# The bounds of a query tile as a stream of their own, and new allowances, in a planned kernel of attention and long convolution

## The chip, the cores and the metric

One core of one Trainium2 chip runs the kernel. The metric is the device time of one execution in microseconds; the time before is 1150.65 us, the median of three runs (1150.41 to 1154.25). TensorE is written PE, VectorE DVE, ScalarE ACT, GpSimd POOL and SyncE SP in the rows.

## The reference, cut to what matters

Two independent layers stand side by side in the output. The first is a state space convolution over 2048 positions and 576 channels, whose kernel is made from 128 complex exponentials per channel. The second is attention with 32 query heads of 18 rows and one key and value head.

```
def _A_ref(u, A_re, A_im, B_re, B_im, C_re, C_im, log_dt, Dskip):
    ...
    P = jnp.exp(logdA[:, :, None] * l[None, None, :])
    K = jnp.einsum("dn,dnl,dn->dl", Cc, P, dB).real
    ...                                   # y = irfft(rfft(u) * rfft(K)), causal, in float32
    y = y.transpose(0, 2, 1) + u * Dskip[None, None, :]

def _B_ref(x, wq, wk, wv, wo):
    q = (x @ wq).reshape(B, S, H, Dh).transpose(0, 2, 1, 3)
    k = x @ wk
    v = x @ wv
    scores = jnp.einsum("bhqd,bkd->bhqk", q, k) * (Dh ** -0.5)
    p = _softmax(scores, axis=-1)
    o = jnp.einsum("bhqk,bkd->bhqd", p, v)
    return o.transpose(0, 2, 1, 3).reshape(B, S, H * Dh) @ wo

return jnp.concatenate([a, b], axis=-1)
```

## The kernel before, in words

**Attention is the main line.** The 2048 queries are cut into 4 chunks `c` of 512 columns. A group `g` is four heads, two pairs; a chunk has eight groups. For each pair and each of 16 key blocks `kb` a score tile `s` of 128 keys by two heads by 512 queries is made by TensorE (`scores`, L516), ScalarE makes the exponential `P` of it (L527; L525 for the first group, with a bias), and a product with the values adds it to the output bank `ops` (L823). There are 1024 such tiles. `main` walks over them in rounds of three, because there are three score tiles (`NS`) in PSUM: in each round it emits three scores, three exponentials, and one or two products of two tiles each, which lag behind; ten `P` tiles (`NP`) lie between. At the end of a group VectorE copies `ops` to `o` (`gather`, through the helper at L123), and the first product of the next group has to wait for that copy, since there is one output bank. The 1024 tiles make 342 rounds, and 32 groups have 31 ends that wait in this way.

**Side work of attention.** A query tile (c, m) holds the projected queries of up to seven heads. `qproj` (matmuls at L408, bank `q`) makes it, and VectorE writes it as two half precision parts `qh` and `ql`; `queries` stores both to DRAM (`qd`) by nine or so DMAs on POOL's queue (L458). Then follows the bound of the tile: a small matrix `aw`, matmuls into the bank `up` (L193), the maximum `un`, its running maximum, and the shift `sh`, which POOL stores too (L496). `fetch` lets SyncE bring the finished operands `aug` of a head pair back from DRAM (L505); the scores of the pair wait for them. There are 20 tiles; the first one, and the key side, are made in `setup`. At the end of a chunk the output is scaled and projected (`outproj`, bank `op`; in the last chunk in parts, bank `part` and `finish`).

**Convolution.** The 576 channels are worked through in 12 blocks `k`. For each block a front stream (VectorE tables `tab`, matmuls `kg`, copy `ksb`) and a back stream (transforms `hu`, `lu`, `hk`, `lk` on TensorE, long products `us`, `ks`, `acc` on VectorE, inverse transform `iy`, L119 is the helper of most of the VectorE work). A back stream runs beside the next front stream. In three places of the program (`powers`, "bursts") ScalarE loads other tables and evaluates sines on `stage` for the following blocks, and makes no exponentials of scores meanwhile.

**What sets the order.** All orders on TensorE, VectorE and ScalarE are written out when the program is built, by a planner with a clock of its own (`Clock`): it counts assumed costs for TensorE (`t`), VectorE (`v`) and ScalarE (`a`). The side work, the preparation of outputs and the convolution are Python generators (`Stream`), which yield a kind, an earliest time, and whether they hold the one bank `f` that all side matmuls share. Kind "p" is matmul work, "v" VectorE work, "w" waits for a condition, "b" is a burst that waits for other side work or 16 steps. After the scores of a round `main` gives it a credit of time, and `fill` lets streams spend it, in a set order of preference, until the next score tile is free by the planner's clock. Constants steer this: `RATE` and `PACE` say how much convolution work a step should have seen, `TOTAL` and `LAST` how much filling is spread over how many steps, `GAP`, `DEFER`, `SLACK`, `HEAD`, `LEFT` shift single decisions. In the kernel before a query tile and its bound are one generator (`yield from self.queries(...)`), so a tile's bound comes before the next tile's projection.

Of the kernel before, what the change touches and what calls it, by code (L numbers as in the profile page):

```python
# [9 lines left out]
F32 = mybir.dt.float32  # L10
# [7 lines left out]
P = 128  # L18
# [12 lines left out]
HQ = (0, 7, 14, 21, 28, 32)  # L31
# [11 lines left out]
NS = 3  # L43
NP = 10


RATE = 1.84
PACE = 1.79
AHEAD = 0.7
TOTAL = 340.0  # L50
LAST = 500

GAP = 0.4
DEFER = 0.5
NAUG = 5
SLACK = 3.0
HEAD = 12

LEFT = 0.85

LATE = {1: [0], 3: [1], 5: [2], 6: [3]}

# [133 lines left out]
class Attention:  # L196
# [36 lines left out]
    def setup(self, tp, conv):  # L233
# [48 lines left out]
        self.outs, self.step, self.due, self.scaled = [], 0, 1 << 30, {}  # L282
        self.o_left = self.q_left = self.units = 0
        self.todo, self.busy, self.group = [], False, 0
        self.side_work = Stream(self.side(), self.k, 99.0)
        conv.begin(6)
        p1, small = (self.ps_s.tile([P, 2, CT], F32, tag="s", name=n) for n in ("first", "small"))
# [21 lines left out]
                queries(p1, j, k)  # L309
            project(p1, 3, 0, 0, k)  # L310
        nc.scalar.activation(h1, p1, AF.Copy, scale=QS)
        self.ab0 = ab = self.p2.tile([P, 2], F32, tag="ab", name="ab0_0")
        V.tensor_reduce(ab[:, 0:1], p1, axis=AX.X, op=ALU.max, apply_absolute_value=True)
        V.scalar_tensor_tensor(l1, p1, QS, h1, op0=ALU.mult, op1=ALU.subtract)
        V.tensor_scalar(ab[:, 0:1], ab[:, 0:1], QS, None, op0=ALU.mult)
# [78 lines left out]
    def qproj(self, c, m, xt):  # L394

        nc, V, K = self.nc, self.V, self.k
        w, nf = self.wq[m], 2 if m < 4 else 1
        self.q_left = 5 * nf
        yield "p", K.fill, False
        ps = self.bank(CT, f"q{c}_{m}")  # L400
        for f in range(nf):
            for k in range(5):
                for j in range(4):

                    o = slice(32 * j, 32 * j + 32)
                    i = o if m < 4 else slice(32 * (j % 2), 32 * (j % 2) + 32)
                    x = slice(256 * f, 256 * f + 256) if m < 4 else slice(256 * (j // 2), 256 * (j // 2) + 256)
                    nc.tensor.matmul(ps[o, 256 * f:256 * f + 256], w[:, k, i], xt[:, k, x], start=(k == 0), stop=(k == 4), tile_position=(0, 32 * j))  # L408
                K.pe(0.465)
                self.q_left -= 1  # L410
                self.units += 1
                if (f, k) != (nf - 1, 4):
                    yield "p", 0.0, True
        self.conv_wait()
        qh, ql, ab = self.operands(c, m)
        n = 256 * nf
        V.tensor_scalar(qh[:, :n], ps[:, :n], QS, None, op0=ALU.mult)
        V.scalar_tensor_tensor(ql[:, :n], ps[:, :n], QS, qh[:, :n], op0=ALU.mult, op1=ALU.subtract)
        K.filled()
        V.tensor_reduce(ab[:, 0:1], qh[:, :n], axis=AX.X, op=ALU.max, apply_absolute_value=True)  # L420
        yield from self.queries(c, m, qh, ql, ab)

    def conv_wait(self):
        self.k.v = max(self.k.v, self.k.t)
# [1 line left out]
    def operands(self, c, m):  # L426
        return (self.p2.tile([P, CT], F16, tag="qh", name=f"qh{c}_{m}", bufs=1),
                self.p2.tile([P, CT], F16, tag="ql", name=f"ql{c}_{m}", bufs=1),
                self.p2.tile([P, 2], F32, tag="ab", name=f"ab{c}_{m}"))

    @staticmethod
    def pieces(m, h0):
# [10 lines left out]
    def queries(self, c, m, qh, ql, ab):  # L443

        nc, V, K = self.nc, self.V, self.k
        h0, h1 = HQ[m:m + 2]
        if m == 0:
            self.qd[c] = self.dr.tile([H, 55, CT], F16, tag="qd", name=f"qd{c}")
        qd = self.qd[c]

        n0 = 4 if (c, m) == (0, 0) else 0

        def store(q):
            for row, src in ((0, qh), (18, qh), (36, ql)):
                for i, h, n, d, nd in self.pieces(m, n0):
                    for f in range(1 if m < 4 else 2):
                        cs, i1 = (slice(0, CT), i) if m < 4 else (slice(256 * f, 256 * f + 256), i + 64 * f)
                        q.dma_start(qd[h:h + n, row + d:row + d + nd, cs], src[i1:i1 + n * nd, :cs.stop - cs.start])  # L458

        def store_first(q):  # L460
            for row, part in ((0, 0), (18, 0), (36, 1)):
                for i, h, d, nd in ((72, 4, 0, 18), (90, 5, 0, 6), (96, 5, 6, 12), (108, 6, 0, 18), (126, 7, 0, 2)):
                    src = self.parts[part + 2 * (i >= 96)]
                    q.dma_start(qd[h, row + d:row + d + nd, :], src[i:i + nd, :])
        (store_first if n0 else store)(nc.gpsimd)
        yield "v", 0.0, False
        while not self.bounded:
            yield "w", 0.0, False
        aw = self.p2.tile([P, P], F32, tag="aw", name=f"aw{c}_{m}")

        ends = (FLOOR, ALU.max) if n0 else (TOP, ALU.min)
        V.tensor_scalar(aw, ab[:, 0:1].broadcast_to([P, P]), ends[0], self.kmax[:, m:m + 1], op0=ends[1], op1=ALU.mult)

        yield "p", max(K.v + (0.4 if self.due < self.step + 12 else SLACK), K.fill), False

        up = self.bank(8, f"up{c}_{m}")
        matmul4(nc, up, aw, self.sel[:, 8 * m:8 * m + 8], stop=(m == 0))
        if m > 0:
            n = 8 if m == 4 else 4
            for b in range(0, n, 4):  # L480
                matmul4(nc, up[:, b:b + 1], self.aw, self.sel[:, 39 + m:40 + m], start=False, stop=(b + 4 == n))
        self.aw = aw
        K.pe(0.1)
        K.v = max(K.v, K.t + 0.3)
        un = self.p2.tile([P, 1], F32, tag="un", name=f"un{c}_{m}", bufs=4)
        V.tensor_reduce(un, up, axis=AX.X, op=ALU.max)
        K.filled()
        if self.ubound is not None:
            u2 = self.p2.tile([P, 1], F32, tag="u2", name=f"u2_{c}_{m}", bufs=4)
            V.tensor_tensor(u2, un, self.ubound, op=ALU.max)  # L490
# [200 lines left out]
    def side(self):  # L691

        xts = {0: self.x0}
        units = [(c, m) for c in range(NCH) for m in range(5)]
        yield from self.queries(0, 0, None, None, self.ab0)
        for c, m in units[1:]:
            self.due = 16 * (8 * c + (0, 1, 3, 5, 7)[m])
            while self.outs:
# [64 lines left out]
    def main(self, conv, flag):  # L763
        nc, K = self.nc, self.k
# [5 lines left out]
        for st in conv.streams:  # L770
            st.ready = 0.0
        prep = Stream(self.prepare(), K, 99.0)
        pairs = [(c, g, kb, j) for c in range(NCH) for g in range(8) for kb in range(16) for j in range(2)]
        state = dict(credit=0.0, filled=0.0)

# [3 lines left out]
        def force(done):  # L779
            while not done():  # L780
                st = holder()
                (side if st is None else st).advance()
                self.fetch(self.group)

        def fill(then):
# [3 lines left out]
            while more:  # L789
# [1 line left out]
                credit = state["credit"] - (K.t - t - idle)  # L791
                urgent = self.due < self.step + 8
                late = self.late()
                for st in (prep, side, conv) if urgent else (prep, conv, side):

                    if st is side and side.kind == "p" and not (urgent or side.holds) and conv.lags(self.step):
                        continue
                    spare = credit - 0.3 if st is not side or urgent or late or side.holds else 0.0
                    wait = then - K.t - (1.2 if st is side and not urgent and not side.holds and self.units > 0.6 * self.step + HEAD else 0.15)
                    if st.go(self.step, max(spare, wait, 0.3 * (st is side and side.holds and conv.lags(self.step) and credit > -1.0)), holder()):  # L800
                        more = True
                        break
                else:

                    at = min((x for x in (st.event() for st in [prep, side] + conv.streams) if x > K.t), default=then)
                    if at < then - 0.5:
                        idle += at - K.t
                        K.t = at
                        more = True
# [1 line left out]
            if K.t > t:  # L811
                K.t += 0.03
            state["filled"] += K.t - t
            state["credit"] = max(state["credit"] - (K.t - t), -0.8)

        def product(n):
            nonlocal o_ps
# [17 lines left out]
        for r in range(0, len(pairs), NS):  # L835
# [24 lines left out]

                self.load_wo()

            state["credit"] = min(state["credit"] + NS / 2 * (0.88 + min(max((TOTAL - state["filled"]) / max(LAST - s, 20), 0.45), 0.7 if s < 384 else 0.9)), 1.2 + 0.88)

            def free():

# [116 lines left out]
class Conv:  # L983
# [303 lines left out]
    def meanwhile(self):  # L1287

        K = self.k
        while K.v < K.t - GAP:  # L1290
            st = min((st for st in self.streams if st.live and st.kind == "v" and st.ready <= K.v and not st.gen.gi_running),
                     key=lambda st: st.work, default=None)
            if st is None or self.work > self.at.step * RATE + 20.0:
                break
            w0 = K.work
            st.advance()
# [151 lines left out]
    def go(self, step, credit, lock):  # L1448
        self.turn()
        lag = step * RATE - self.work  # L1450
        if lag < -20.0:
            return False
        ahead = AHEAD + min(max(lag, 0.0) / 20.0, 1.0)
        for st in self.streams:
# [121 lines left out]
```

## Time and profile before

| what | us |
|---|---|
| median of 3 runs (lowest, highest) | 1150.65 (1150.41, 1154.25) |
| span of the profiled execution, first to last instruction | 1153.0 |
| busy: TensorE matmuls, VectorE, ScalarE, GpSimd | 1083.5, 987.4, 998.8, 140.6 |
| first exponential of scores starts | 26.87 |
| last exponential of scores ends | 1128.27 |

The page gives no other time for the profiled execution than its span. Busy shares are the union of an engine's instruction times; matmuls overlap each other in their tails, so the busy time of TensorE is more than what its instructions need one after the other. A float32 matmul of the program leaves two records. Rows of an engine carry in square brackets how long it was idle before them and what ended that.

### The profile page before, as it was taken

Reading aid. Unit: us, or ns where it says so; the run is one execution under the profiler, and the core shown is the slowest. Engines: PE = TensorE matmul, PEld = TensorE weight load, DVE = VectorE, ACT = ScalarE, POOL = GpSimd, SP = SyncE. Lnnn points to the kernel's source line nnn. Section 1 sums busy time; section 2 is a strip of 40 time slices with the busy share of each in tenths; the row PEclk is TensorE's granted clock in tenths of the full one; section 3 lists DMA queues with packets and bytes.
Section 4 is the critical chain, followed back from the end, with each engine's and each line's share of the span. In section 5 each row is a group of like instructions: output and inputs, shape, how many; then the busy total and the mean of one; then the engine's idle time right before and its main releaser. Section 6 shows DMA issues by size and latency. Waiting matters only on the chain.

```text
span 1153.0 us, 33012 instructions
## 1 busy us (share of the span) xinstructions
PE 1083.5 (94%) x13886; PEld 395.9 (34%) x13886; DVE 987.4 (86%) x1679; ACT 998.8 (87%) x1052; POOL 140.6 (12%) x257
## 2 busy tenths in 40 slices
PE   6999899989999999989999999999998999999998
PEld 2333233333333334323333333333332333332423
DVE  3697997998997897897799899898699799799694
ACT  2888979879989898998998899988999988899891
POOL 5232320112032000001021200001040000000000
PEclk9899999999999999999999999999999999999999
DMA  7422242114122202112222300202221301301201
GB/s 224 130 57 84 76 133 89 45 41 135 32 67 78 74 29 88 45 63 93 82 79 71 110 21 28 93 28 85 75 78 46 111 20 39 106 19 54 77 33 58
DMA packets 59279, 83.37 MB, mean 72 GB/s; under 512 B 14867, under 2 KB 35335, under 8 KB 58613
## 3 DMA queue, kind: packets, MB, share of 16 engines
q1 hardware_dynamic: 47557, 73.24, 19.4%
q0 software_dynamic: 10848, 7.37, 2.6%
q8 instruction: 111, 1.82, 0.6%
q10 hardware_dynamic: 720, 0.58, 0.2%
q14 instruction: 43, 0.35, 0.1%
HBM read 46.59 MB, written 33.85 MB: 70 GB/s over the span
## 4 chain that ended last, share of the span: by engine, by line
PE 64%; DVE 15%; ACT 14%; issue 5%; DMA 1%; SPq 0%; ACTq 0%; DVEq 0%
PE ops L823 27%; PE s L516 17%; ACT P L527 12%; PE op L193 5%; PE q L408 3%; DVE tab L119 3%; PE kg L1257 3%; PE iy L193 3%; DVE ks L119 1%; DVE acc L119 1%; DVE t L119 1%; PE hk L193 1%; PE fin L193 1%; PE lk L193 1%; DMA xr<-xT 1%
## 5 line engine op out<-in xcount | busy, mean ns | idle before, releaser
L527 ACT ACTIVATE P<-s 128x1024 f32<-128x1024 f32 x992 | 934.8, 1034 | 104.6 <-PE s L516 102.2
L823 PE MATMUL ops<-P,v_sb 128*32 128x512 f32 x4096 | 513.0, 601 | 8.5 <-DVE o L123 8.4
L516 PE MATMUL s<-aug,kaug 55*128 55x512 f16 x2048 | 309.9, 384 | 36.6 <-ACT P L527 30.7
L516 PEld LDWEIGHTS <-kaug 55*128 55x128 f16 x2048 | 92.2, 94 | 371.7 <-issue 328.5
L823 PEld LDWEIGHTS ops<-P,v_sb 128*32 128x32 f32 x4096 | 117.2, 110 | 162.6 <-issue 126.1
L458 POOL DMA_DIRECT2D qd<-qh x116 | 65.7, 573 | 323.2 <-DVE qh L127 320.6
L408 PE MATMUL q<-x,wq_sb 128*32 128x256 f32 x1360 | 84.2, 382 | 3.2 <-DVE sck L119 2.5
L193 PE MATMUL op<-wo_sb,oT 126*32 126x288 f32 (+1 forms) x1048 | 74.8, 410 | 2.6 <-DVE sck L119 1.2
L119 DVE TENSOR_TENSOR tab<-tab,tt 128x576 f32<-128x576 f32 (+1 forms) x72 | 59.1, 821 | 1.4
L123 DVE COPY ksb<-kg 128x192 f32<-128x192 f32 x48 | 17.5, 364 | 49.1 <-PE kg L1257 48.9
L119 DVE TENSOR_TENSOR tt<-fr,sum 128x576 f32<-128x576 f32 (+1 forms) x72 | 58.9, 818 | 0.0
L119 DVE TENSOR_TENSOR tab<-tab 128x576 f32<-128x576 f32 (+1 forms) x72 | 58.9, 818 | 0.0
L119 DVE TENSOR_TENSOR tab<-fr,dif 128x576 f32<-128x576 f32 (+1 forms) x72 | 58.9, 818 | 0.0
L119 DVE TENSOR_TENSOR tab<-sum,fr 128x576 f32<-128x576 f32 (+1 forms) x72 | 58.8, 816 | 0.0
L408 PEld LDWEIGHTS q<-x,wq_sb 128*32 128x32 f32 x1360 | 40.5, 110 | 43.4 <-issue 19.1
L1168 POOL MEMSET fr<- 128x192 f32 x24 | 9.8, 494 | 323.8 <-DVE tt L119 225.2
L119 DVE TENSOR_TENSOR acc<-acc,pt 128x1728 f32<-128x1728 f32 (+2 forms) x36 | 48.7, 1352 | 0.3
L119 DVE TENSOR_TENSOR pt<-us,ks 128x1728 f32<-128x1728 f32 (+2 forms) x36 | 48.2, 1351 | 0.0
L525 ACT ACTIVATE P<-s,bias 128x1024 f32<-128x1024 f32 x32 | 32.7, 1131 | 15.1 <-PE s L516 15.1
L193 PEld LDWEIGHTS op<-wo_sb,oT 126*32 126x32 f32 (+1 forms) x1048 | 29.8, 110 | 42.2 <-issue 17.4
L1257 PEld LDWEIGHTS kg<-tab 128*32 128x32 f32 x2304 | 35.5, 110 | 22.9 <-issue 7.9
L1257 PE MATMUL kg<-tab 128*32 128x64 f32 x2304 | 41.8, 221 | 1.5 <-DVE ksb L123 1.1
(160 smaller groups left out, 1018.0 us busy)
## 6 DMA issues: line engine op xcount, KB each, us to landing
od<-o SPq DMA_DIRECT2D x31, 256.0 KB
aug<-qd SPq DMA_DIRECT2D x124, 55.0 KB
u<-u SPq DMA_DIRECT2D x12, 384.0 KB
kd<-ksb SPq DMA_DIRECT2D x12, 384.0 KB
kt<-kd SPq DMA_DIRECT2D x48, 96.0 KB
outa<-u SPq DMA_DIRECT2D x12, 384.0 KB
pw<-pw SPq DMA_DIRECT2D x8, 528.0 KB
oT<-od SPq DMA_DIRECT2D x16, 252.0 KB
```

The lines of the kernel that those rows point to most:

```text
L119: return self.v.tensor_tensor(out, *a, **k)
L123: return self.v.tensor_copy(out, *a, **k)
L193: nc.tensor.matmul(ps[j:e], w[:, j:e], x, start=start, stop=stop, tile_position=(0, j))
L408: nc.tensor.matmul(ps[o, 256 * f:256 * f + 256], w[:, k, i], xt[:, k, x], start=(k == 0), stop=(k == 4), tile_position=(0, 32 * j))
L458: q.dma_start(qd[h:h + n, row + d:row + d + nd, cs], src[i1:i1 + n * nd, :cs.stop - cs.start])
L516: nc.tensor.matmul(ps[:, j, :], self.kaug[r, kb * P:(kb + 1) * P], t[r, :], start=True, stop=True)
L525: nc.scalar.activation(pt, ps, AF.Exp, bias=self.bias, scale=SCALE / QQ)
L527: nc.scalar.activation(pt, ps, AF.Exp, scale=SCALE / QQ)
L823: nc.tensor.matmul(o_ps[32 * j:32 * j + 32, :], self.v[:, kb, :], pts[2 * n + j // 2][:, j % 2, :], start=(kb == 0), stop=(kb == 15), tile ...
L1168: nc.gpsimd.memset(t[:, :, 0:NF:8], one)
L1257: nc.tensor.matmul(ps[32 * g:32 * g + 32, d, :], t[:, :32], t[:, 32:], start=(j == 0), stop=(j == 1), tile_position=(0, 32 * g))
```

## The change

The bound of a tile leaves `queries` and becomes a method of its own, `bound`. `queries` now only issues the stores and appends the bound to a list, `tails`. A new stream, `tail`, works through this list; the side stream goes on with the next tile. In `fill` the tail stream stands behind the preparation and before side work and convolution, and has a fixed allowance of 1.0. `ab` gets six buffers, as several tiles may wait for their bounds. The pair of convolution streams stays. The constants are set anew, and twelve that stood in the code as numbers become `C1` to `C12` (two lines of the table are shown). The convolution may be 47.793 us of VectorE work ahead of its pace instead of 20.

```diff
-TOTAL = 340.0
-LAST = 500
+TOTAL = 429.151
+LAST = 560.514
...
-        yield from self.queries(c, m, qh, ql, ab)
+        self.queries(c, m, qh, ql, ab)
+        yield "v", 0.0, False
...
         (store_first if n0 else store)(nc.gpsimd)
+        self.tails.append(self.bound(c, m, ab, n0, qd))
+
+    def tail(self):
+
+        while True:
+            if self.tails:
+                yield from self.tails.pop(0)
+            else:
+                yield "w", 0.0, False
+
+    def bound(self, c, m, ab, n0, qd):
+
+        nc, V, K = self.nc, self.V, self.k
+        h0, h1 = HQ[m:m + 2]
         yield "v", 0.0, False
         while not self.bounded:
             yield "w", 0.0, False
...
         def force(done):
             while not done():
                 st = holder()
-                (side if st is None else st).advance()
+                if st is None:
+                    st = tail if self.tails or tail.kind != "w" else side
+                st.advance()
...
-                for st in (prep, side, conv) if urgent else (prep, conv, side):
+                for st in (prep, tail, side, conv) if urgent else (prep, tail, conv, side):
...
-                    spare = credit - 0.3 if st is not side or urgent or late or side.holds else 0.0
-                    wait = then - K.t - (1.2 if st is side and not urgent and not side.holds and self.units > 0.6 * self.step + HEAD else 0.15)
+                    spare = 1.0 if st is tail else credit - C9 if st is not side or urgent or late or side.holds else 0.0
+                    wait = then - K.t - (C6 if st is side and not urgent and not side.holds and self.units > C7 * self.step + HEAD else C8)
...
-            state["credit"] = min(state["credit"] + NS / 2 * (0.88 + min(max((TOTAL - state["filled"]) / max(LAST - s, 20), 0.45), 0.7 if s < 384 else 0.9)), 1.2 + 0.88)
+            state["credit"] = min(state["credit"] + NS / 2 * (0.88 + min(max((TOTAL - state["filled"]) / max(LAST - s, 20), C1), C2 if s < 384 else C3)), C4 + 0.88)
...
         lag = step * RATE - self.work
-        if lag < -20.0:
+        if lag < -C11:
             return False
```

Three places of the orders are shown. The first is VectorE's order near the start, where the queries of tiles 1 and 2 of the first chunk become `qh` and `ql` and the shift `sh` of tile 1 is made. Before:

```order
L127 TENSOR_SCALAR qh_1_627<-q_1_533 128x512
L131 SCALAR_TENSOR_TENSOR ql_1_628<-q_1_533,qh_1_627 128x512
L135 TENSOR_REDUCE ab_1_629<-qh_1_627 128x1
L127 TENSOR_SCALAR aw_1_642<-ab_1_629,kmax 128x128
L119 TENSOR_TENSOR tt_0_0_0_593<-fr_423,sum_542 128x576
L119 TENSOR_TENSOR tab_0_590<-tab_0_590 128x24x24
L135 TENSOR_REDUCE un_1_678<-up_1_669 128x1
L119 TENSOR_TENSOR u_0_1_680<-un_1_678,un_0_499 128x1
L127 TENSOR_SCALAR sh_1_682<-u_0_1_680 8x256
```

Of the change:

```order
L128 TENSOR_SCALAR qh_2_712<-q_2_618 128x512
L132 SCALAR_TENSOR_TENSOR ql_2_713<-q_2_618,qh_2_712 128x512
L136 TENSOR_REDUCE ab_2_714<-qh_2_712 128x1
L136 TENSOR_REDUCE un_1_744<-up_1_735 128x1
L120 TENSOR_TENSOR u_0_1_746<-un_1_744,un_0_584 128x1
L128 TENSOR_SCALAR sh_1_748<-u_0_1_746 8x256
```

The shift of tile 1 has moved from behind its own tile to behind the queries of tile 2. The second place is POOL's queue at the same point, where `qd` is the buffer in DRAM. Before:

```order
L458 DMA qd_353<-ql_1_628 16x512
L458 DMA qd_353<-ql_1_628 6x18x512
L458 DMA qd_353<-ql_1_628 4x512
L496 DMA qd_353<-sh_1_682 7x2x256
L458 DMA qd_353<-qh_2_808 14x512
L458 DMA qd_353<-qh_2_808 6x18x512
```

Of the change:

```order
L461 DMA qd_353<-qh_2_712 6x512
L461 DMA qd_353<-ql_2_713 14x512
L461 DMA qd_353<-ql_2_713 6x18x512
L461 DMA qd_353<-ql_2_713 6x512
L513 DMA qd_353<-sh_1_748 7x2x256
L513 DMA qd_353<-sh_2_819 7x2x256
```

The store of `sh` of tile 1 has moved behind the nine stores of tile 2, and stands right before that of tile 2. The third place is TensorE's order at the end of group 5 of the first chunk, where the product stream goes from bank `ops_5` to `ops_6` (weight loads, and the second matmul of each score tile and of the bound, are left out). Before:

```order
L516 MATMUL s_12_2_3103<-aug_112,kaug 128x512
L516 MATMUL s_13_2_3106<-aug_113,kaug 128x512
L823 MATMUL ops_5_2729<-P_10_15_3018,v_sb 32x512 x2
L823 MATMUL ops_5_2729<-P_11_15_3020,v_sb 32x512 x2
L823 MATMUL ops_6_3125<-P_12_0_3054,v_sb 32x512 x2
L823 MATMUL ops_6_3125<-P_13_0_3056,v_sb 32x512 x2
```

Of the change:

```order
L846 MATMUL ops_5_2830<-P_10_15_3118,v_sb 32x512 x2
L846 MATMUL ops_5_2830<-P_11_15_3120,v_sb 32x512 x2
L194 MATMUL up_4_3167<-sel_sb,aw_4_3122 32x8 x4
L533 MATMUL s_13_1_3187<-aug_113,kaug 128x512
L533 MATMUL s_12_2_3190<-aug_112,kaug 128x512
L533 MATMUL s_13_2_3193<-aug_113,kaug 128x512
L410 MATMUL q_0_3203<-x_3095,wq_sb 32x256 x20
L533 MATMUL s_12_3_3228<-aug_112,kaug 128x512
L533 MATMUL s_13_3_3231<-aug_113,kaug 128x512
L533 MATMUL s_12_4_3234<-aug_112,kaug 128x512
L410 MATMUL q_0_3203<-x_3095,wq_sb 32x256 x16
L846 MATMUL ops_6_3262<-P_12_0_3149,v_sb 32x512 x2
```

Between the last product of one group and the first of the next there is now a bound, scores and a projection.

## Rows read from the trace of the kernel before

**Rows 1.** Page, part 1: busy us (share) xinstructions of each engine.

```profile
PE 1083.5 (94%) x13886; PEld 395.9 (34%) x13886; DVE 987.4 (86%) x1679; ACT 998.8 (87%) x1052; POOL 140.6 (12%) x257
```

**Rows 2.** Waits: engine, line <- whom: us in total, times, longest us.

```profile
ACT P L527 <- PE s L516: 102.2, 186, 2.4
...
PE ops L823 <- DVE o L123: 8.4, 8, 2.3
```

**Rows 3.** Stretches: us, busy (x) by engine, granted clock, DMA share, GB/s.

```profile
93.50:162.30 68.80, 60.62 (x688) 20.88 (x686) 65.01 (x110) 61.90 (x64) 14.55 (x23) 0.95 0.33 104
...
26.40:1126.80 1100.40, 1046.21 (x13420) 380.22 (x13416) 969.63 (x1642) 990.39 (x1041) 127.37 (x230) 0.99 0.22 69
```

**Rows 4.** Chain of waits near 107 us: start us, us, what.

```profile
107.19 0.75 PE s L516 x6
...
108.73 0.86 PE ops L823 x8
```

**Rows 5.** Page, part 5, the exponentials: busy, mean ns | idle before, releaser.

```profile
L527 ACT ACTIVATE P<-s 128x1024 f32<-128x1024 f32 x992 | 934.8, 1034 | 104.6 <-PE s L516 102.2
```

**Rows 6.** Timeline 53 to 68 us: start us, us, engine, line, instruction [idle before].

```profile
52.96 9.15 ACT L525 ACTIVATE P<-s,bias 128x1024 f32<-128x1024 f32 x9 [1.44 <-PE s L516]
53.22 1.07 PE L408 MATMUL q<-x,wq_sb 128*32 128x256 f32 x16
...
55.35 3.37 POOL L458 DMA_DIRECT2D qd<-qh  x6 [10.14 <-DVE qh L127]
...
57.34 0.28 PE L193 MATMUL up<-sel_sb,aw 128*32 128x8 f32 x16
...
59.47 1.94 PE L408 MATMUL q<-x,wq_sb 128*32 128x256 f32 x32
60.35 0.60 POOL L496 DMA_DIRECT2D qd<-sh  x1
...
63.58 3.13 SPq L505 DMA_DIRECT2D aug<-qd  x7
...
66.53 0.82 PE L516 MATMUL s<-aug,kaug 55*128 55x512 f16 x6
```

**Rows 7.** The instructions on the tile `sh`: its stores' time to landing.

```profile
DMA to landing us min/median/max: 1.7/2.3/6.2
```

**Rows 8.** Timeline 247 to 256 us, an end of a group.

```profile
247.58 0.82 PE L516 MATMUL s<-aug,kaug 55*128 55x512 f16 x6
...
248.34 1.06 PE L823 MATMUL ops<-P,v_sb 128*32 128x512 f32 x8
...
249.65 1.35 DVE L119 TENSOR_TENSOR pt<-us,ks 128x1152 f32<-128x1152 f32 x1
...
251.66 1.07 PE L823 MATMUL ops<-P,v_sb 128*32 128x512 f32 x8 [2.26 <-DVE o L123]
...
252.66 1.46 PE L516 MATMUL s<-aug,kaug 55*128 55x512 f16 x6
...
253.35 2.86 ACT L527 ACTIVATE P<-s 128x1024 f32<-128x1024 f32 x3 [2.42 <-PE s L516]
...
254.04 2.50 PE L823 MATMUL ops<-P,v_sb 128*32 128x512 f32 x12
```

**Rows 9.** Timeline 136.5 to 147 us, TensorE after the first burst.

```profile
140.01 0.60 PE L516 MATMUL s<-aug,kaug 55*128 55x512 f16 x2 [2.00 <-ACT P L527]
...
142.38 3.64 PE L823 MATMUL ops<-P,v_sb 128*32 128x512 f32 x16
```

**Rows 10.** Stretch behind the first burst, columns as in rows 3.

```profile
140.00:145.00 5.00, 4.37 (x22) 0.90 (x21) 5.00 (x8) 4.54 (x5) 2.38 (x5) 0.51 0.33 91
```

**Rows 11.** Timeline 832 to 841 us, the third burst.

```profile
832.91 1.28 ACT L1125 ACT_TABLE_LOAD   x1
...
835.74 4.52 PE L408 MATMUL q<-x,wq_sb 128*32 128x256 f32 x80 [1.24 <-DVE sck L119]
...
838.55 2.85 ACT L527 ACTIVATE P<-s 128x1024 f32<-128x1024 f32 x3
```

More of the change, by code (lines that the diff above doesn't have):

```diff
@@ L44 @@
 NP = 10
-RATE = 1.84
-PACE = 1.79
-AHEAD = 0.7
-TOTAL = 340.0
-LAST = 500
-GAP = 0.4
-DEFER = 0.5
+RATE = 1.829
+PACE = 1.71
+AHEAD = 0.752
+TOTAL = 429.151
+LAST = 560.514
+GAP = 0.437
+C1, C2, C3, C4, C5, C6, C7, C8, C9, C10, C11, C12 = 0.529, 1.112, 0.728, 0.947, 0.591, 0.827, 0.566, 0.187, 0.25, 0.502, 47.793, 16.067
+DEFER = 0.48
 NAUG = 5
-SLACK = 3.0
-HEAD = 12
-LEFT = 0.85
+SLACK = 3.096
+HEAD = 8.716
+LEFT = 0.638
 LATE = {1: [0], 3: [1], 5: [2], 6: [3]}
@@ L284, in setup @@
         self.todo, self.busy, self.group = [], False, 0
+        self.tails = []
         self.side_work = Stream(self.side(), self.k, 99.0)
@@ L311, in setup @@
         nc.scalar.activation(h1, p1, AF.Copy, scale=QS)
-        self.ab0 = ab = self.p2.tile([P, 2], F32, tag="ab", name="ab0_0")
+        self.ab0 = ab = self.p2.tile([P, 2], F32, tag="ab", name="ab0_0", bufs=6)
         V.tensor_reduce(ab[:, 0:1], p1, axis=AX.X, op=ALU.max, apply_absolute_value=True)
@@ L428, in operands @@
                 self.p2.tile([P, CT], F16, tag="ql", name=f"ql{c}_{m}", bufs=1),
-                self.p2.tile([P, 2], F32, tag="ab", name=f"ab{c}_{m}"))
+                self.p2.tile([P, 2], F32, tag="ab", name=f"ab{c}_{m}", bufs=6))
     @staticmethod
@@ L694, in side @@
         units = [(c, m) for c in range(NCH) for m in range(5)]
-        yield from self.queries(0, 0, None, None, self.ab0)
+        self.queries(0, 0, None, None, self.ab0)
+        yield "v", 0.0, False
+        while not self.bounded:
+            yield "w", 0.0, False
         for c, m in units[1:]:
@@ L772, in main @@
         prep = Stream(self.prepare(), K, 99.0)
+        tail = Stream(self.tail(), K, 99.0)
         pairs = [(c, g, kb, j) for c in range(NCH) for g in range(8) for kb in range(16) for j in range(2)]
@@ L803, in fill @@
                 else:
-                    at = min((x for x in (st.event() for st in [prep, side] + conv.streams) if x > K.t), default=then)
-                    if at < then - 0.5:
+                    at = min((x for x in (st.event() for st in [prep, tail, side] + conv.streams) if x > K.t), default=then)
+                    if at < then - C10:
                         idle += at - K.t
@@ L813, in fill @@
             state["filled"] += K.t - t
-            state["credit"] = max(state["credit"] - (K.t - t), -0.8)
+            state["credit"] = max(state["credit"] - (K.t - t), -C5)
         def product(n):
@@ L1292, in meanwhile @@
                      key=lambda st: st.work, default=None)
-            if st is None or self.work > self.at.step * RATE + 20.0:
+            if st is None or self.work > self.at.step * RATE + C11:
                 break
```

## The prediction

> **What bounds the kernel now.** I read the busy shares first [rows 1]: TensorE 94%, ScalarE 87%, VectorE 86%, so no engine rules alone. Next comes who waits for whom [rows 2]: ScalarE stands still for 102.2 us because a score tile has not come, and TensorE waits 8.4 us, in 8 waits, for the copy that empties the output bank at the end of a head group. Then the stretches [rows 3]. From the first exponential to the last full round are 1100.4 us, 341 rounds, which I cut into 18 stretches of 19; in them ScalarE is busy for 990.4 and VectorE for 969.6.
>
> The chain of waits [rows 4] gives what TensorE really needs apiece: 0.75 us for the scores of a round, 0.86 for one product. With such net times, the tail of the last matmul left out, all of TensorE's work in the 341 rounds makes about 950 us, well under its busy time in the same stretch (1046.2, [rows 3]), which counts the tails of overlapping matmuls. An exponential takes 934.8/992 = 0.94 us [rows 5], so ScalarE needs 2.83 us per round and TensorE 950/341 = 2.79. The mean round lasts 1100.4/341 = 3.23. Two engines with equal mean loads hand over through three score tiles, so whatever is uneven from round to round is lost on one side or the other. That loss, about 0.4 us per round, is what a new order can win or add to; the totals stay.
>
> **The change part by part.** No arithmetic is added or removed; only positions move. Three places carry the sum, with the evenness of the rounds and the end of a group.
>
> *Startup, a loss.* The bound of a tile (`up`, `un`, `sh`) is now a stream of its own, so the next tile can overtake it. The order shows that at tile 1: `sh` of tile 1 now stands behind `qh` and `ql` of tile 2 on VectorE, and behind their nine stores on POOL's queue. Before, it stood ahead of them. Its price follows from the same steps of the earlier tile [rows 6]. The projection ends at 53.22 + 1.07 = 54.29, the first store is issued at 55.35, nine of them hold the queue until `sh` goes at 60.35, and SyncE fetches the operands at 63.58, that is 9.3 us after the projection ended. The scores that use them start at 66.53, unhindered, so the data is there at most 12.2 us after that end; with the quickest landing of such a store, 1.7 instead of about 3.2 [rows 7], it would be some 1.5 earlier, and where the fetch too lands at once, at 9.8. I take 11.5, nearer to the bound that was seen. In the changed order the scores of pair 3 open round 11. Between the end of tile 2's projection and them lie two products with an `up` (2.0 us) and rounds 9 and 10, at 3 x 1.02 = 3.05 each in this early part (nine exponentials in 9.15, [rows 6]): 8.1 us. Matmuls wait 3.4 us (bounds 1.7 to 4.1), and as ScalarE has little left in its tiles, I count 3. The projections are also moved into rounds 2 to 4, but that work only comes earlier.
>
> After such a stand TensorE's clock has fallen here: it stood 2.26 us before 251.66 and 2.00 before 140.01 [rows 8, 9], and after the latter the granted clock was 0.51 in 140 to 145 [rows 10], nearly all of it at the lower of its two levels, 1.2 GHz. At the first of the two, scores took 1.46 instead of 0.82 and twelve records of products 2.50 instead of 1.49 (1.06 for eight and half of 0.86), 1.7 us in all; at the other sixteen took 3.64 instead of 1.06 + 0.86, again 1.7. I add 1.5, so startup loses 4.5 (0 to 7). The Trainium skill, "TensorE: Matmul & The Clock Gate", section "HAM oscillation — how this bites in real kernels", says that matmul work broken by waits is throttled again after the break and must warm up anew. By that rule this wait and the one at the third burst below are each followed by a slow spell, as the sum has it; without any spell the sum would be 3.5 us better.
>
> *Group ends, a gain.* At the end of a group the product stream changes its bank and must wait for VectorE's copy of the old one. Before, the last product of group 5 and the first of group 6 stand next to each other; the copy comes behind a convolution product of 1.35 us, TensorE stands 2.26 us and ScalarE then 2.42 [rows 8]. Counted over the 31 ends of a group in the order of each program, five had less than 0.35 us of other matmul work in between; now the least is 0.66, and the sum grows from 36 to 50 us. At this very place two rounds of scores and 36 projection matmuls are put in. Of the 8.4 us [rows 2] I let 3 remain: -5.5, and the slow spell after 249.4 goes, -1.7: together -7 (0 to -10).
>
> *First burst, a gain.* In each of three bursts ScalarE evaluates sines for the convolution and makes no exponentials. In the first, TensorE had 36 projection matmuls (of two records each) and one product, ran dry, and the slow spell followed [rows 9]. Now the same round has 40 and two products, by 0.44 (32 records take 1.94, 16 take 1.07, [rows 6]) + 0.86 = 1.3 us more. The stand of 2.00 shrinks to 0.7, and the spell may go: 1.3 + 1.7 = 3, so -3 (0 to -3.5).
>
> *Third burst, a loss.* There before had 80 records of projection, 4.52 us, beside ScalarE's 832.91 to 838.55 [rows 11]. All projections are done by round 179 now, and by the order this round has scores and three products, 0.75 + 3 x 0.86 = 3.3 us, beside 5.6 without exponentials. The stand itself costs little, as ScalarE is the one that is late; a slow spell behind it would cost about what the other two did: +2 (0 to 4).
>
> *Evenness, a gain.* With the net times, rounds that hold just scores and one product fall from 26 to 12. Summed over threes of rounds, the larger of TensorE's and ScalarE's work falls from 1019.7 to 1012.0. VectorE's share of the crowded second stretch falls from 65 to 62 us by the same count of its instructions; that stretch took 68.8, with VectorE busy for 65.0, against a mean of 61.1 for the 18 stretches (1100.4/18, [rows 3]). The two falls are 7.7 and 3; I take half of them, -5.2, between nothing and -11.
>
> Sum: +4.5 - 7 - 3 + 2 - 5.2 = -8.7. The stores of `sh` are otherwise not late: the other bounds have 22 or more rounds until their heads are due. Six buffers of `ab` and the list of waiting bounds cost no time on the chip. The tail I cost at nothing: one last inverse transform leaves it, and three output products enter; both lie on TensorE.
>
> The profiled span is 1153.0, 2.35 above the median of 1150.65; the profile gives no other time for that execution. The span would become 1144.3, and a median of the same offset 1142.0.
>
> **Rivals.** *VectorE comes late (slower).* The convolution may now run 47.8 us of VectorE work ahead of its pace, instead of 20. In the order 15.9 and 12.8 us of VectorE work stand ahead of two group copies (rounds 247 and 257) with nothing in them that waits for TensorE; before, the most was 10.6. If copies thus come 0.9 us later each on the mean, 31 of them take 28 us, two thirds of it with ScalarE dry, as its 2.42 stood beside TensorE's 2.26 at the one place: +18 - 8.7, about 1160. It decides from a mean delay of 0.42, where it eats the sum. For it speaks VectorE's 65.0 of 68.8 us in the second stretch [rows 3]; against it, that this stretch gets lighter and VectorE is ahead of before's count at nearly every round.
>
> *Nothing moves.* The 8.4 us and the unevenness become waits at other places, because all three totals are as before; only startup and third burst remain, against the first burst and half the group ends: about 1150. For it: ScalarE's 102.2 us [rows 2] are spread over 186 waits, few of which I can name.
>
> *The startup wait does not come.* The wait on tile 1 needs the write of `sh` to take as long as before: it landed at most 3.2 us after 60.35, the median of all twenty is 2.3 and the least 1.7 [rows 7]. With 1.7, quick fetches and no spell, +4.5 becomes 1, and where evenness pays in full (-11) the sum is -18: 1133. The Trainium skill, "DMA: Bandwidth & Descriptors", section "Anatomy of one DMA — SWDGE (gpsimd) path", gives such a transfer about 2.0 us of fixed cost, most of it the confirmation that the write landed; by that, an estimate, the wait would be about 1.2 us shorter than with the 3.2 seen.
>
> **How the numbers follow.** The forecast gets 0.48 (its own range 1134 to 1150), late VectorE 0.13, nothing moves 0.19, no startup wait 0.20. About half a per cent, 5.75 us, is what a measurement of this kernel tells from no change: faster means under 1144.9, slower over 1156.4. Faster: 0.35 of the forecast and all of the last rival, 0.55. Same: 0.13 of the forecast and 0.15 of "nothing moves", 0.28. Slower: late VectorE and the rest, 0.17. The range, 1127 to 1157, leaves out a little of both ends.
>
> **What would show it.** Startup: a stand of about 3 us of TensorE before scores near 70 us, ended by the fetch of operands, with a granted clock below 1.00 behind it; none, and the first step is wrong. Group ends: waits of products on the copy `o` under 4 us in all. First burst: clock 1.00 behind it. Third burst: no projection beside it, TensorE standing for 2 to 3 us, ScalarE not. Evenness: ScalarE's wait for scores down from 102 to about 90. I would be wrong if those waits stay near 102, or if waits of TensorE on VectorE grow.

## The result, and the profile after

The changed kernel takes 1153.72 us (median of 20 runs) against 1152.01 us before (20 runs): ratio 1.0019, 95% interval [1.0011, 1.0027]. It is slower by about 1.7 us, where 1142 was forecast. One run of the kernel before, at 1362.5 us, was in a slower state and is left out of the ratio.

Busy time is as before [rows 1]; page, part 1, of the changed kernel:

```profile
PE 1085.5 (94%) x13886; PEld 398.2 (35%) x13886; DVE 988.2 (86%) x1676; ACT 997.1 (87%) x1052; POOL 140.1 (12%) x257
```

The waits of the changed kernel (engine, line <- whom: us in total, times, longest):

```profile
ACT P L544 <- PE s L533: 96.9, 166, 2.1
...
ACT P L542 <- PE s L533: 13.3, 7, 7.9
...
DVE oT L120 <- DMA db<-rden: 5.2, 1, 5.2
...
PE fin L194 <- DVE flag L918: 4.9, 1, 4.9
...
PE ops L846 <- DVE o L124: 2.4, 5, 0.6
...
PE s L533 <- DMA aug<-qd: 1.7, 1, 1.7
```

ScalarE waits less for scores (96.9 against 102.2, [rows 2]) and the group copies are nearly free (2.4 against 8.4). New are the third, the fourth and the last row, of one wait each: VectorE stands 5.2 us for a DMA, TensorE 4.9 us for VectorE, and scores wait 1.7 us for operands near the start. Where the first two are, the timeline shows, from the last exponential `P` on (start us, us, engine, line, instruction [idle before]):

```profile
1119.28 1.02 ACT L544 ACTIVATE P<-s 128x1024 f32<-128x1024 f32 x1 [0.24 <-PE s L533]
...
1120.24 0.20 DVE L128 TENSOR_SCALAR dn<-dn 28x128 f32<-28x128 f32 x1
...
1122.79 0.77 SPq L580 DMA_DIRECT2D db<-rden  x1
1126.62 0.69 DVE L120 TENSOR_TENSOR oT<-oT,db 126x512 f32<-126x512 f32 x1 [5.19 <-DMA db<-rden]
...
1127.29 0.40 DVE L675 TENSOR_SCALAR rc_last<-ops 128x256 f32<-128x256 f32 x1
1127.36 4.07 PE L194 MATMUL fin<-wo_sb,oT 126*32 126x288 f32 x32 [4.87 <-DVE flag L918]
```

The kernel before at the same place:

```profile
1113.20 0.21 DVE L127 TENSOR_SCALAR dn<-dn 28x128 f32<-28x128 f32 x1
...
1126.42 0.68 DVE L119 TENSOR_TENSOR oT<-oT,db 126x512 f32<-126x512 f32 x1
...
1127.25 1.02 ACT L527 ACTIVATE P<-s 128x1024 f32<-128x1024 f32 x1 [0.46 <-PE s L516]
...
1131.41 3.10 PE L193 MATMUL fin<-wo_sb,oT 126*32 126x288 f32 x48
```

The last exponential ends 8.0 us earlier than before (1120.30 against 1128.27), about what the whole forecast was. But the last quarter of the output's preparation (`dn`, its reciprocal, the trip through DRAM, the multiply into `oT`) is over at the same time as before, 1127.3 against 1127.1. It used to be done 1.2 us ahead of the last exponential's end; now it starts when that one ends. Everything behind it on VectorE waits, and TensorE stands 4.87 us. The tail, from the last exponential's end to the end of the span, grows from 24.7 to 31.3 us.

Why is it late? The four parts of the last chunk's preparation are one generator, and each takes the planner's 8 + 5 + 7 us. By the program they can't begin before the output of chunk 2 has left `oT`. Its last copy `ob` was at 1038.76 and is at 1044.75 now, though the exponentials run 6 to 8 us ahead; what delays it is not shown. The first `dn` moved from 1048.0 to 1055.6, the others follow at 21 to 22 us, and the last one comes 65 us behind the first in both kernels.

A profile can also mislead in itself. The two spans differ by -1.4 us (1153.0 to 1151.6), the medians by +1.7. The execution of the profile after took 1153.4 us, 1.8 more than its span, and so in each later profile (1.76 to 1.86). By that, as an estimate, the profiled execution of the kernel before took some 1154.8, 2.8 over its median, while the prediction carried the span to the median by an offset of -2.35. That of the change lies 0.3 under its own median. A slow start may be part of the 2.8: the last section shows the same start at full clock.

### The profile page after: what moved, and what is told of

It reads as the page before. It is cut to its first block, busy times and chain, and to the rows that moved or that the text cites. A ratio compares the mean times of both kernels' runs of the same rounds, so it can differ in the third digit from the quotient of the medians.

```text
span 1151.6 us, 33003 instructions
## 1 busy us (share of the span) xinstructions
PE 1085.5 (94%) x13886; PEld 398.2 (35%) x13886; DVE 988.2 (86%) x1676; ACT 997.1 (87%) x1052; POOL 140.1 (12%) x257
## 4 chain that ended last, share of the span: by engine, by line
PE 63%; ACT 16%; DVE 11%; issue 6%; DMA 2%; POOL 1%; ACTq 0%; DVEq 0%
PE ops L846 25%; PE s L533 17%; ACT P L544 14%; PE op L194 5%; PE q L410 3%; PE kg L1280 3%; PE iy L194 3%; DVE tab L120 2%; PE fin L194 1%; POOL qd L461 1%; PE hk L194 1%; DVE ks L120 1%; DVE acc L120 1%; PE lu L194 1%; PE lk L194 1%
## 5 line engine op out<-in xcount | busy, mean ns | idle before, releaser
L544 ACT ACTIVATE P<-s 128x1024 f32<-128x1024 f32 x992 | 933.0, 1035 | 99.3 <-PE s L533 96.9
L120 DVE TENSOR_TENSOR ks<-ks 128x576 f32<-128x576 f32 (+1 forms) x48 | 41.0, 855 | 0.9
```

The costliest lines, as they stand in the source:

```text
L120: return self.v.tensor_tensor(out, *a, **k)
L544: nc.scalar.activation(pt, ps, AF.Exp, scale=SCALE / QQ)
```

## The experiments

Ten profiles, with main line from the start of the first exponential to the end of the last, ScalarE's waits for scores, and tail, in us. Each ratio is to runs of the kernel before of the same set; their median was 1152.05 for e1 to e4 and 1153.35 for e5 to e8, so medians of different sets compare less well than ratios. The last three columns are of one execution each; that of e8 took 1175.7 us, 7.7 over its median.

| kernel | time (median) | ratio to before [95%] | main line | waits | tail |
|---|---|---|---|---|---|
| before | 1152.0 | 1 | 1101.4 | 117.3 | 24.7 |
| the change | 1153.7 | 1.0019 [1.0011, 1.0027] | 1094.6 | 110.2 | 31.3 |
| e1 change, short waits | 1146.2 | 0.9958 [0.9943, 0.9973] | 1094.5 | 110.3 | 24.0 |
| e2 before, short waits | 1151.8 | 0.9999 [0.9986, 1.0012] | 1102.5 | 116.4 | 23.7 |
| e3 constants alone | 1155.8 | 1.0039 [1.0026, 1.0053] | 1105.2 | 122.4 | 23.9 |
| e4 stream alone | 1164.8 | 1.0128 [1.0107, 1.0148] | 1115.3 | 133.2 | 19.2 |
| e5 before, longer waits | 1158.5 | 1.0048 [1.0029, 1.0068] | 1096.8 | 102.6 | 33.7 |
| e6 = e1, shift on other queue | 1144.2 | 0.9930 [0.9906, 0.9954] | 1090.4 | 107.6 | 23.9 |
| e7 = e1, bound first at start | 1152.0 | 0.9999 [0.9982, 1.0016] | 1099.5 | 114.9 | 24.9 |
| e8 = e1, one rate back | 1168.0 | 1.0135 [1.0108, 1.0161] | 1121.3 | 137.0 | 26.2 |

The waits have in them one of 7.9 to 9.9 us ahead of the first exponential, outside the main line; in e5 alone it is booked as a wait for VectorE. Without it, main line less waits is 991 to 994 us in all ten. So the main line is ScalarE's own work plus its waits for scores, and those waits are what an order changes.

**e1 and e2: the preparation's planned waits.** The same edit in the changed kernel (e1) and in the one before (e2):

```diff
-        yield "v", K.t + 8.0, False
+        last = c == NCH - 1
+        yield "v", K.t + (4.0 if last else 8.0), False
...
-        yield "v", max(K.v, K.t) + 5.0, False
+        yield "v", max(K.v, K.t) + (1.0 if last else 5.0), False
...
-            yield "v", K.t + 7.0, False
+            yield "v", K.t + (5.0 if last else 7.0), False
```

> The changed kernel; only the planned waits of the preparation of the last chunk's output are shortened (8, 5 and 7 us become 4, 1 and 5), so that each of its four parts takes about 10 us instead of 20. Nothing before about 1045 us moves. Theory 'end chain': in the changed kernel the last exponential ends 8.0 us earlier than before (1120.3 against 1128.3), but the four parts of that preparation follow each other from 1055.6 to 1126.6, and everything behind the multiply at 1126.6 waits; then TensorE's stand of 4.87 us and the slow 32 records behind it (4.07 instead of 2.08) go, the tail behind the last exponential falls from 31.3 to 24 to 25 us, and the time by 5 to 8 us to about 1147. Rival 'more output products': the tail is longer because 192 instead of 168 output products are left for it; the stand goes but its work comes anyway, and the time falls by under 2 us. Rival 'scatter': the earlier end of the main line is an accident of one execution; the last exponential ends near 1127 here too, and the time stays at 1152 to 1154.

> The kernel before with the same shortened waits of the last chunk's preparation. Theory 'end chain': there the multiply at 1126.4 comes before the last exponential ends at 1128.3 and nothing waits for it, so the time stays within 1.5 us of before. Rival 'shorter waits are better anywhere': it falls by 4 us or more, as in the changed kernel, since more output products go into the main line.

e1 is 7.5 us faster than the change and 0.42% faster than before. Its timeline at the end:

```profile
1106.47 0.68 DVE L120 TENSOR_TENSOR oT<-oT,db 126x512 f32<-126x512 f32 x1
...
1119.53 1.02 ACT L544 ACTIVATE P<-s 128x1024 f32<-128x1024 f32 x1 [0.24 <-PE s L533]
...
1121.58 3.10 PE L194 MATMUL fin<-wo_sb,oT 126*32 126x288 f32 x48
```

The multiply is done 13 us ahead of the last exponential, the stand and the slow records behind it are gone, VectorE's only wait for such a DMA is 0.9 us, and the tail is 24.0. The main line is the same in this second execution (1094.5), so "scatter" falls. As many output products are left as in the change (192 records), so "more output products" falls too. In e2 the time stays, as expected, though only 128 records are left instead of 168: there nothing waited for the multiply.

**e3 and e4: the two halves of the change.** e3 runs the bound inside the side stream again, with all new constants; e4 keeps the new stream with the constants of before:

```diff
         self.queries(c, m, qh, ql, ab)
-        yield "v", 0.0, False
+        yield from self.tails.pop(0)
...
         self.queries(0, 0, None, None, self.ab0)
-        yield "v", 0.0, False
-        while not self.bounded:
-            yield "w", 0.0, False
+        yield from self.tails.pop(0)
```

```diff
-RATE = 1.829
+RATE = 1.84
...
-C1, C2, C3, C4, C5, C6, C7, C8, C9, C10, C11, C12 = 0.529, 1.112, 0.728, 0.947, 0.591, 0.827, 0.566, 0.187, 0.25, 0.502, 47.793, 16.067
+C1, C2, C3, C4, C5, C6, C7, C8, C9, C10, C11, C12 = 0.45, 0.7, 0.9, 1.2, 0.8, 1.2, 0.6, 0.15, 0.3, 0.5, 20.0, 16.0
...
```

> The changed kernel with all its new constants, but the bound of a tile is again part of the side stream, ahead of the next tile's projection. Theory 'constants': the earlier end of the main line comes from the new allowances (convolution up to 47.8 us ahead, projections done early); it ends near 1120 to 1122 here too. Rival 'stream': it comes from the bounds beside the next tile; it ends near 1127 or later. In both, the scores near 66 us wait no more for the operands of tile 1, as sh of tile 1 is stored ahead of the queries of tile 2: 1 to 2 us less there. The end of the program depends on when the last chunk's preparation begins, so the comparison is that of the last exponential, not of the time alone.

> The bound as a stream of its own, as in the change, but all constants as before. Theory 'constants': the main line ends no earlier than before, 1127 or later, and the time is 1152 to 1156. Rival 'stream': it ends at 1120 to 1123, and the time is 1145 to 1148 if the last chunk's preparation is not the last to end. Both expect a wait of scores for the operands of tile 1 near 66 us, 1 to 3 us.

Both theories fall: each half alone makes the main line longer than before, by 3.8 and 13.9 us, and only together they shorten it, by 6.8. e3's loss is rather some 3 us larger, as its start had full clock and was 3.3 us ahead at the 33rd exponential. The gain can't be divided between the halves, as each half alone gives another plan. The wait of scores for operands near 66 us, which both had expected of e4, did not come (0.2 us in the whole run). The largest single loss in each is TensorE waiting for VectorE's part of the convolution, first e3, then e4:

```profile
562.89 1.33 PE L194 MATMUL hu<-u,dft_sb 128*32 128x192 f32 x16 [3.50 <-DVE scu L120]
```

```profile
93.48 1.51 PE L1280 MATMUL kg<-tab 128*32 128x64 f32 x48 [3.67 <-DVE tab L120]
```

In the whole changed kernel such waits (`kg`, `hu`, `lk`, `lu` on VectorE) come to 1.2 us.

**e5: the mend turned round.** The kernel before with longer planned waits:

```diff
-        yield "v", K.t + 8.0, False
+        last = c == NCH - 1
+        yield "v", K.t + (10.0 if last else 8.0), False
...
-        yield "v", max(K.v, K.t) + 5.0, False
+        yield "v", max(K.v, K.t) + (6.5 if last else 5.0), False
...
-            yield "v", K.t + 7.0, False
+            yield "v", K.t + (8.5 if last else 7.0), False
```

> The kernel before with longer planned waits of the last chunk's preparation (8, 5, 7 us become 10, 6.5, 8.5: 25 for each of the four parts instead of 20), so that its last multiply moves from 1126.4 behind the last exponential at 1128.3. It is the mend of the changed kernel turned round. Theory 'end chain': the last multiply then comes 6 to 8 us behind the last exponential, the tail grows from 24.7 to 29 to 32 us, TensorE stands for 2 to 5 us in it, and the time rises by 4 to 7 us to 1156 to 1159. Rival 'more output products': only what is left to multiply with the output weights counts, the tail grows by 1 to 3 us, without a stand.

```profile
1121.22 1.02 ACT L527 ACTIVATE P<-s 128x1024 f32<-128x1024 f32 x1 [0.46 <-PE s L516]
...
1130.74 0.69 DVE L119 TENSOR_TENSOR oT<-oT,db 126x512 f32<-126x512 f32 x1 [5.60 <-DMA db<-rden]
...
1131.49 5.99 PE L193 MATMUL fin<-wo_sb,oT 126*32 126x288 f32 x48 [5.40 <-DVE oT L119]
```

The kernel before gets the same wound: VectorE waits 5.60 us for the DMA, TensorE 5.40, and the 48 records behind take 5.99 instead of 3.10. The tail is 33.7, 9.0 us longer and more than the 29 to 32 expected. The time is 0.48% longer, 5.1 us between the medians; 1.1 us is won in the last 64 exponentials, and where the rest of the 9.0 goes is not shown. The rival expected no stand, and only 8 records more of output products are left (176 against 168), so it falls. "End chain" stands from both sides.

**e6: the shift's store leaves the crowded queue.**

```diff
-        nc.gpsimd.dma_start(qd[h0 + n0:h1, 54, :]...
+        (nc.sync if (c, m) == (0, 1) else nc.gpsimd).dma_start(qd[h0 + n0:h1, 54, :]...
```

> As the changed kernel with short waits, and the store of sh of tile 1 of the first chunk goes out on SyncE's queue instead of GpSimd's, so that it no longer stands behind the nine stores of tile 2. No instruction of TensorE, VectorE or ScalarE moves. Theory 'startup wait': the store goes at about 60 us instead of 63.6, the scores near 69 us no longer wait for operands (1.56 us before), the slow spell behind that wait goes too, and the time falls by 2 to 4 us, to 1142 to 1144. Rival 'hidden': the wait only takes the place of one on ScalarE, which was late anyway; exponential 96 and all later ones end within 1 us of where they did.

First the changed kernel at this place, then e6:

```profile
62.67 0.60 POOL L513 DMA_DIRECT2D qd<-sh  x1
...
66.43 0.95 PE L533 MATMUL s<-aug,kaug 55*128 55x512 f16 x5 [1.66 <-DMA aug<-qd]
...
68.59 1.92 PE L846 MATMUL ops<-P,v_sb 128*32 128x512 f32 x8
```

```profile
60.29 0.28 SPq L513 DMA_DIRECT2D qd<-sh  x1
...
65.43 1.15 PE L533 MATMUL s<-aug,kaug 55*128 55x512 f16 x6
...
67.20 1.04 PE L847 MATMUL ops<-P,v_sb 128*32 128x512 f32 x8
```

The wait is gone and the time is 2.1 us less than e1's. The eight product records at 1.04 us instead of 1.92 are not this edit's doing: in e1 they took 1.04 too, behind a wait of 1.56. In the two profiles e6 leads e1 by 4.5 us at the 64th exponential, counted from the first one's start; 2.9 of it is there at the 33rd, the last one ahead of the wait; the clock in 30 to 40 us was 1.00 in e6 and 0.50 in e1. So the wait was worth about 1.6 us, and 1.2 of it is left at the end (4.1 less 2.9): "hidden" falls. The two ratios come from two sets of runs and their intervals overlap, so the runs alone don't settle the size. It is the fastest version of the study: 0.70% faster than before, with the change kept.

**e7 and e8: what a new plan does.** e7 holds the projection of tile 2 back until the bound of tile 1 is through; e8 sets one rate back:

```diff
...
+            while (c, m) == (0, 2) and (self.tails or self.bounding):
+                yield "w", 0.0, False
```

```diff
-RATE = 1.829
+RATE = 1.84
```

> As the changed kernel with short waits, and the projection of tile 2 of the first chunk is held back until the bound of tile 1 is through. Everything planned behind it comes out in a new order. Theory 'startup wait': no scores wait for operands near 68 us; exponential 64 ends 3 to 5 us earlier. Theory 'each plan by itself': what follows is planned anew and can come out better or worse by several us whatever the start; the last exponential lies anywhere from 1112 to 1128. Rival 'only the start counts': the gain at exponential 64 is still there at the last one, and the time is 1141 to 1143.

> As the changed kernel with short waits, and one constant, the rate of the convolution's work, set back from 1.829 to 1.84 (0.6%). The order is the same up to about 300 us and differs in a good third of its rows behind it. Theory 'each plan by itself': the main line's end moves by 3 to 12 us, up or down, though nothing of the mechanism changed. Rival 'evenness by design': it moves by less than 2 us, as so small a change of a rate leaves the plan as good as it was.

In e7 no scores wait for these operands, and the 64th exponential ends 71.8 us after the start of the first, 5.9 us sooner than in e1; 2.9 of that is there at the 33rd, as the slow clock at the start was shorter in that execution (0.95 and 0.70 in 30 to 40 us against 0.50). At the last one it is 5.0 us behind, so "only the start counts" falls. In e8 a rate moved by 0.6% costs 21.8 us between the medians and 20 by the two ratios, far more than the 3 to 12 of "each plan by itself". First a stretch of its timeline with one of its losses, then the row of its waits at the group ends:

```profile
1097.58 0.69 DVE L120 TENSOR_TENSOR oT<-oT,db 126x512 f32<-126x512 f32 x1 [6.07 <-DMA db<-rden]
...
1098.79 1.46 PE L194 MATMUL lu<-u,dft_sb 128*32 128x192 f32 x16 [3.59 <-DVE scu L124]
1100.18 1.46 PE L533 MATMUL s<-aug,kaug 55*128 55x512 f16 x6
1100.89 1.94 ACT L544 ACTIVATE P<-s 128x1024 f32<-128x1024 f32 x2 [4.81 <-PE s L533]
```

```profile
PE ops L847 <- DVE o L124: 10.3, 8, 2.5
```

This loss begins at the multiply, whose planned waits e1 had shortened: VectorE stands 6.07 us at it until its operand has come through DRAM, and the copy `scu` behind it is late for TensorE. In e1 the one such wait is 0.9 us. So a planned wait can be too short as well as too long.

e3, e4, e7 and e8 all have a longer main line than the plan that they were made from, the changed kernel or e1. Two readings are open: each new plan is a draw from a wide spread, or the new constants fit each other and any step away loses.

## Why the prediction was wrong

**The step that failed** is the sentence on the tail, "The tail I cost at nothing", with its reason, "one last inverse transform leaves it, and three output products enter; both lie on TensorE". It counted matmuls. That count was right: 192 records of output products against 168, the inverse transforms at 1107 to 1112 instead of 1127 to 1132. What it did not ask is when the operands of these products come. A chain through two DMAs and VectorE, paced by planned waits, has its last `dn` 74 to 76 us behind chunk 2's output in both kernels, so a main line that ends earlier runs into it. The price is 6.6 us of tail (31.3 - 24.7) and 7.5 us by e1. The order before the run showed it: the last `dn` stood behind the last inverse transform's sum, with hardly an instruction left behind it to hide the trip.

**The main line** was forecast at -8.7. The two profiles show -6.8, or -8.0 for the end of the last exponential. As the profiled execution of the kernel before lies well over its median, the medians fit a smaller gain: +1.7 with 6.6 lost in the tail leaves -4.9, and e1's ratio gives -4.8 (0.0042 x 1152), of which 0.7 is its shorter tail. So the sign held, at about half the size; ScalarE's wait for scores fell to 96.9, not to about 90. Term by term, from the two profiles:

*Startup (+4.5):* the wait came as told, `sh` behind nine stores and TensorE waiting for the fetch, but 1.66 us instead of 3. Up to the 64th exponential the change is 2.7 us behind (76.9 against 74.2 from the first one's start), e1 3.5. Another loss of about 3 us was left out. Between profiles with like clock at the start, the changed order is behind at the 33rd exponential already: e1 by 2.9 (41.8 against 38.9 of before, both about 0.50 to 0.58 in 30 to 40 us), e6 by 3.3 (38.9 against 35.6 of e5, both 1.00). There the projections stand that the change moved into rounds 2 to 4, of which the prediction says "that work only comes earlier". At the 96th exponential, behind the first burst, 1.4 and 0.2 us of it are left (e6 has no wait for operands). First e5, where ScalarE makes 21 exponentials without a stand, then e6 in the same stretch, with three stands:

```profile
25.43 21.38 ACT L525 ACTIVATE P<-s,bias 128x1024 f32<-128x1024 f32 x21 [8.04 <-DVE km L135]
```

```profile
35.78 1.05 PE L410 MATMUL q<-x,wq_sb 128*32 128x256 f32 x16
...
37.19 3.13 ACT L542 ACTIVATE P<-s,bias 128x1024 f32<-128x1024 f32 x3 [0.93 <-PE s L533]
...
40.72 3.13 ACT L542 ACTIVATE P<-s,bias 128x1024 f32<-128x1024 f32 x3 [0.41 <-PE s L533]
...
45.06 3.12 ACT L542 ACTIVATE P<-s,bias 128x1024 f32<-128x1024 f32 x3 [1.21 <-PE s L533]
```

The slow spell behind the wait came in the change (clock 0.70 in 65 to 70 us) and not in e1, after a wait of 1.56 (1.00). The Trainium skill, "TensorE: Matmul & The Clock Gate", section "HAM oscillation — how this bites in real kernels", tells of matmul work throttled anew behind each wait for a DMA, with longer waits than here. Here one wait of two was followed by a slow spell, so to cost a spell as certain was too much (the stretch 65 to 70 us of the change, then of e1; columns as in [rows 3]):

```profile
65.00:70.00 5.00, 3.57 (x61) 1.88 (x64) 0.40 (x2) 2.85 (x3) 0.60 (x1) 0.70 0.31 85
```

```profile
65.00:70.00 5.00, 3.44 (x44) 0.95 (x47) 2.10 (x6) 3.15 (x4) 1.73 (x4) 1.00 0.23 65
```

*Group ends (-7):* the waits came out right, 2.4 us left where 3 were forecast. What that was worth is measured at one place only: at that of [rows 8] the 32 exponentials of the group take 34.3 us instead of 37.3, with a projection where the stand was:

```profile
242.48 1.92 PE L846 MATMUL ops<-P,v_sb 128*32 128x512 f32 x16
...
245.29 2.37 PE L410 MATMUL q<-x,wq_sb 128*32 128x256 f32 x40
...
250.09 1.90 PE L846 MATMUL ops<-P,v_sb 128*32 128x512 f32 x16
```

*First burst (-3):* right, at -3.4. The stand is 0.98 instead of 2.00 [rows 9], the clock behind it 1.00 instead of 0.51 [rows 10], and 24 exponentials around it take 28.9 us instead of 32.3.

```profile
131.05 0.39 PE L533 MATMUL s<-aug,kaug 55*128 55x512 f16 x2 [0.98 <-ACT P L544]
```

*Third burst (+2):* the events came, the price did not. TensorE stands 2.42 us for ScalarE and the clock falls to 0.70 in 850 to 855 us and 0.61 in the next 5, but the 64 exponentials around it take 67.9 us against 67.8 with the projections of [rows 11].

```profile
851.35 0.39 PE L533 MATMUL s<-aug,kaug 55*128 55x512 f16 x2 [2.42 <-ACT P L544]
...
858.00 4.69 ACT L544 ACTIVATE P<-s 128x1024 f32<-128x1024 f32 x5 [2.12 <-PE s L533]
```

*Evenness (-5.2):* what is left of -6.8 is -3.2 (-6.8 - 2.7 + 3.0 + 3.4 - 0.1), the other group ends with it. It is no steady gain: from exponential 416 to 544 the change loses 8 us against before, from there to the end it wins 9.8. Four other plans (e3, e4, e7, e8) have a main line 5 to 27 us longer than the change's, so a new plan moves the sum of many small waits by as much as the tally and more. Half of one (7.7 and 3, so 5.4 rather than 5.2) was a guess with the right sign; that the sign held is luck, as far as these runs show.

**The rivals.** "VectorE comes late" had its premise wrong: with the allowance C11 alone back at 20 the program comes out the same, row for row, so the new 47.8 us change nothing. But its mechanism is part of what the bad plans lose by: TensorE's waits for the group copies are 8.8 us in e3, 3.7 in e4 and 10.3 in e8, against 2.4. "Nothing moves" had the time nearly right (1150), for a reason that was not the reason: the gain was there and was given back in one place, the tail. The startup wait did come, so the third rival falls.

## What to carry to other kernels

When a change makes the main line end earlier, look for what ends the program and does not move with it: follow the last operands back through their DMAs and planned waits, and ask when that chain starts. A tail is costed by its latest operand, not by a count of its matmuls. Where a planner writes the order, one edited constant can move the time by more than the effect under study (here by 20 us), so mechanisms are tested by edits that leave the order alone, as e6 did, or leave it alone up to the place in question, as e1 and e5 did. And two profiles are compared from a point where their clocks are alike, not from the start of the program.

## What was not expected of the hardware

The same program can start with TensorE at half clock or not. In the profile of before the granted clock is 0.58 and 0.50 in the two stretches from 30 to 40 us; in e5, the same program up to about 1040 us, it is 1.00, and the 33rd exponential ends at 61.0 us instead of 65.7. Of that lead 1.4 us is there before the first exponential (25.43 against 26.87), with clock 1.00 in both, so 3.3 go with the slow clock. The lead, 4.9 us by then, is still there at exponential 928. First before, then e5:

```profile
30.00:35.00 5.00, 4.75 (x23) 2.06 (x22) 0.86 (x6) 5.00 (x6) 2.77 (x6) 0.58 0.34 103
35.00:40.00 5.00, 5.00 (x29) 1.54 (x33) 3.93 (x16) 2.72 (x4) 0.00 (x0) 0.50 0.48 120
```

```profile
30.00:35.00 5.00, 4.09 (x36) 1.94 (x36) 1.67 (x11) 4.93 (x6) 2.67 (x6) 1.00 0.37 102
35.00:40.00 5.00, 4.61 (x48) 1.17 (x46) 4.79 (x11) 5.00 (x6) 0.00 (x0) 1.00 0.65 184
```

e1 and e6, the same program but for one store at about 60 us, differ likewise (0.50 against 1.00). This is as large as the whole effect under study, and could explain why the 19 timed runs of before spread over 7 us (1148.2 to 1155.3). Later runs of it fit: eight with a mean granted clock of 0.997 took 1148.3 to 1152.1 us, six with 0.992 or less 1154.1 to 1157.3. Where in those runs the clock was low is not recorded, and what decides it stays open.
